# The last 128 columns of the attention tiles and of w4, computed turned

## The chip, the cores and the metric

The kernel runs on one core of a Trainium2 chip. The core has TensorE (PE) for matrix products into PSUM (8 banks of 512 float32 columns on 128 partitions), VectorE (DVE), ScalarE (ACT), GpSimd (POOL) and SyncE (SP), which here only starts transfers. The metric is the device time of one execution in microseconds (us). Three runs of the kernel before gave a median of 263.45 us (263.12 to 265.74).

## The reference

Input x has S = 2048 tokens of D = 640 features; all inputs and the output are bf16.

```
g  = sigmoid(sum(x * gate_w))                     # one number per token
q, k, v = x @ wqkv, in 32 heads of 20             # branch A
pq, pk  = phi(q), phi(k)                          # phi(t) = (t + 1 if t > 0 else exp(t)) + 1e-6
a  = (pq (pk^T v) / (pq sum(pk) + 1e-6)) @ wo
h  = gelu(layernorm(x) @ w1), shifted by 1, -1, 2, -2 tokens in four groups of features   # branch B
x1 = x + h @ w2
b  = x1 + gelu(layernorm(x1) @ w3) @ w4           # w3 is 640 x 1728, w4 is 1728 x 640
out = g * a + (1 - g) * b
```

The kernel multiplies (pk^T v) and wo into one 640 x 640 matrix M, so that branch A ends in a = pqn @ M, with pqn the scaled pq.

## The kernel before

Tokens go in 16 tiles of 128, and in 4 chunks of four tiles. The weights and x stay in SBUF. The first part makes q, k and the gate, then M; the second is w1, w2 and the two layernorms; the last part, which the change touches, is w3, the attention tiles and w4.

A matmul takes a stationary operand of up to 128 columns, loaded ahead by an instruction of its own (PEld in the profile), and streams up to 512 columns of the moving operand through it. Of a product of 640 columns that is computed with the tokens as the stationary side, 512 columns go into one PSUM bank and the last 128 into another.

- `w3_group(c, j)` makes 128 of the 1728 features of one chunk with the weights as the stationary side and 512 tokens moving; ScalarE takes the gelu into h2T (bf16, features on the partitions). 1728 is 13 x 128 + 64; the last 64 features of two chunks are made together by `w3_half` and lie in h2h, one tile on partitions 0 to 63 and the next on 64 to 127.
- `a_tile(t)` (line 1085): POOL writes (1 - g) * x1 of one tile into a slot of abx (four slots of 640 float32), TensorE makes pqn @ M for the tile with 5 matmuls of 512 columns and 5 of 128 (recorded at line 613, the helper mm_group), and one sum on VectorE (line 652) adds g times that into abx.
- `w4_half(t)` (line 1098) opens a chunk of w4: it takes three pairs of banks, one bank for the 512 columns of each of the four tiles and two banks for their last 128 columns, and writes the product of the 64 features there (lines 1115 and 1118). Two such matmuls on the lower and the upper partitions use different halves of the rows of the array.
- `w4_tile(t)` (line 1122) adds 13 matmuls of 512 and 13 of 128 columns (line 1136); two sums on VectorE (line 652) then write (1 - g) * psum + abx into x_tok, from where `out_tiles` stores groups of tiles.

The order of the program is made at build time by a planner (`_Items.run`): items stand in streams, each with things that must be placed first, a cost model says when each would be ready, and the earliest ready item goes next; among equals one that has no cost on TensorE, then the one with the longest chain of costs behind it. Each engine gets a list in that order and works through it strictly, waiting on counters of the other engines; TensorE doesn't wait for its own counter. PSUM banks are chosen at build time too, by `bank()` and `pair()`, as the ones that the cost model frees first. All transposes by DMA and nearly all stores are issued from SP's list.

In the trace the last part runs: w3 of chunks 0 and 1 with the first attention tiles in it; then for each chunk c the half block and four w4 tiles, each followed by the attention tile four ahead; between chunks stands w3 of the chunk after next. An attention tile t from 4 on is placed after w4 tile t - 4 (line 1230). The last attention tile, 15, stands between w4 tiles 14 and 15.

## Time and profile before

| | |
|---|---|
| runs of the kernel | 263.45 us median, 263.12 to 265.74 |
| the profiled execution | 262.97 us |
| its span, first to last instruction | 260.9 us |
| TensorE busy, matmuls | 257.1 us, 1651 instructions |
| VectorE, ScalarE, GpSimd busy | 149.1, 107.2, 97.3 us |
| granted TensorE clock | 1.000 |

The profile is of one execution. A row of a group names the line, the engine, the operation, output and inputs with shapes, how often it ran, busy time, mean nanoseconds of one, and the idle time before it with what ended it. A line can be that of a helper: every product made by mm_group has line 613, every sum by stt line 652. A single matmul's recorded duration (379 ns for 512 columns) includes its way through the array, which overlaps the next one; the time from one start to the next is read from the chain in order of time or from the timeline. In the chain a row is the start, the length and the work, with the number of instructions that were merged.

### The profile page before, as it was taken

The page shows a single profiled execution, that of the slowest core. Times are in us where ns is not written, and L with a number is a line of the kernel's source. Part 1 is how long each engine was busy: PE and PEld are TensorE (multiplying, and loading weights), DVE is VectorE, ACT ScalarE, POOL GpSimd, SP SyncE. Part 2 cuts the span into 40 slices and gives each one's busy share as a digit, 9 for nine tenths or more (in the row PEclk, how much of TensorE's full clock was granted, in tenths as well). Part 3 has the DMA queues.
Part 4 walks back from the last instruction along what each step waited for, and adds up shares of the span by engine and source line. Part 5 has one row for each costly group of instructions (what it writes and reads, how often), then busy time and mean ns, then how long its engine had stood idle before and what let it go on. Part 6 is the DMA issues. An engine that isn't in the chain of part 4 may idle for free.

```text
span 260.9 us, 4205 instructions
## 1 busy us (share of the span) xinstructions
PE 257.1 (99%) x1651; PEld 133.0 (51%) x1651; DVE 149.1 (57%) x267; ACT 107.2 (41%) x216; POOL 97.3 (37%) x150
## 2 busy tenths in 40 slices
PE   8999999999999999999999999999999999999996
PEld 3555555544455555555444545554455544455553
DVE  2497887899903799979993407991033410143333
ACT  1396677751365757674974240005500045100000
POOL 5013995859964017958763202320011200011000
PEclk9999999999999999999999999999999999999999
DMA  7755999652766991363585610232000020000211
GB/s 205 247 90 139 171 206 156 172 108 50 102 126 126 333 353 36 71 78 59 102 125 111 122 25 0 47 92 65 0 3 0 0 103 0 0 3 0 101 53 50
DMA packets 51283, 24.98 MB, mean 96 GB/s; under 512 B 42644, under 2 KB 49853, under 8 KB 51264
## 3 DMA queue, kind: packets, MB, share of 16 engines
q1 hardware_dynamic: 49824, 21.15, 36.8%
q0 software_dynamic: 1152, 3.28, 5.4%
q8 instruction: 13, 0.21, 0.3%
q10 hardware_dynamic: 288, 0.30, 0.3%
q14 instruction: 6, 0.05, 0.1%
HBM read 12.04 MB, written 2.62 MB: 56 GB/s over the span
## 4 chain that ended last, share of the span: by engine, by line
PE 97%; DMA 1%; DVE 1%; issue 0%
PE ps L613 61%; PE ps L1136 21%; PE ps L811 7%; PE ps L887 2%; PE ps L791 1%; DMA x_tok<-in_A_x_dram 1%; PE ps L1050 1%; PE ps L1118 1%; DVE x_tok L652 1%; PE ps L964 1%; PE ps L888 1%; PE ps L624 0%; PE ps L792 0%; DVE xT L678 0%; PE ps L1115 0%
## 5 line engine op out<-in xcount | busy, mean ns | idle before, releaser
L613 PE MATMUL ps<-xnT,w 128*128 128x512 bf16 x360 | 82.3, 379 | 0.0
L1136 PE MATMUL ps<-w,h2T 128*128 128x512 bf16 (+1 forms) x416 | 58.8, 299 | 0.0
L669 ACT ACTIVATE h2T<-ps 128x512 bf16<-128x512 f32 x52 | 30.4, 598 | 66.5 <-PE ps L613 66.5
L613 PEld LDWEIGHTS ps<-xnT,w 128*128 128x128 bf16 x360 | 34.0, 98 | 37.4 <-issue 0.4
L652 DVE SCALAR_TENSOR_TENSOR x_tok<-ps,stg,abx 128x512 bf16<-128x512 f32 (+1 forms) x32 | 17.2, 550 | 61.6 <-PE ps L1136 61.6
L635 POOL TENSOR_SCALAR abx<-x_tok,stg 128x640 f32<-128x640 bf16 x16 | 14.8, 928 | 99.6 <-DVE x_tok L652 95.1
L1136 PEld LDWEIGHTS ps<-w,h2T 128*128 128x128 bf16 x416 | 32.4, 98 | 25.6 <-issue 1.1
L635 POOL TENSOR_SCALAR xn<-x_tok,st 128x640 bf16<-128x640 bf16 x32 | 38.9, 1222 | 14.5 <-DMA xnT<-xn 14.0
L669 ACT ACTIVATE Er<-ps 128x640 bf16<-128x640 f32 x32 | 22.4, 706 | 18.1 <-PE ps L613 8.5
L668 ACT ACTIVATE junk<-x_tok 128x640 bf16<-128x640 bf16 x32 | 23.6, 738 | 3.7 <-DVE x_tok L650 3.2
L669 ACT ACTIVATE hsT<-ps 128x512 bf16<-128x512 f32 (+1 forms) x32 | 18.9, 594 | 14.7 <-PE ps L613 14.3
L613 PE MATMUL ps<-M_sb,pqnT 128*128 128x512 bf16 (+1 forms) x160 | 24.3, 299 | 0.0
L613 PE MATMUL ps<-w,hsT 128*128 128x512 bf16 (+1 forms) x160 | 23.9, 299 | 0.0
L652 DVE SCALAR_TENSOR_TENSOR abx<-ps,stg,abx 128x640 f32<-128x640 f32 x16 | 14.1, 884 | 15.8 <-PE ps L613 15.8
L613 PE MATMUL ps<-wkg,xT 128*128 128x512 bf16 (+1 forms) x150 | 22.6, 299 | 0.0
L613 PEld LDWEIGHTS ps<-w,hsT 128*128 128x128 bf16 x160 | 13.3, 98 | 12.3
L613 PEld LDWEIGHTS ps<-M_sb,pqnT 128*128 128x128 bf16 x160 | 13.1, 98 | 10.4
L613 PE MATMUL ps<-wq,xT 128*128 128x512 bf16 (+1 forms) x120 | 18.3, 299 | 0.0
L811 PE MATMUL ps<-pk_tok,x_tok 128*128 128x512 bf16 x80 | 17.8, 379 | 0.0
L650 DVE SCALAR_TENSOR_TENSOR x_tok<-ps,x_tok 128x640 bf16<-128x640 f32 x16 | 13.1, 821 | 6.9 <-PE ps L613 6.0
L635 DVE TENSOR_SCALAR Er<-Er 128x640 bf16<-128x640 bf16 x32 | 11.8, 369 | 8.6 <-ACT Er L669 8.3
L613 PEld LDWEIGHTS ps<-wkg,xT 128*128 128x128 bf16 x150 | 12.1, 97 | 9.0
(74 smaller groups left out, 236.2 us busy)
## 6 DMA issues: line engine op xcount, KB each, us to landing
w<-in_B_w_dram SPq DMA_DIRECT2D x1, 2160.0 KB, 8.2
w<-in_B_w_dram SPq DMA_DIRECT2D x1, 2080.0 KB, 14.9
x_tok<-in_A_x_dram SPq DMA_DIRECT2D x3, 640.0 KB, 5.9
out_dram<-x_tok SPq DMA_DIRECT2D x3, 640.0 KB, 3.2
w<-in_B_w_dram POOLq DMA_DIRECT2D x8, 160.0 KB, 4.8
wkg<-in_A_wqkv_dram SPq DMA_DIRECT2D x5, 160.0 KB, 4.3
wv<-in_A_wqkv_dram POOLq DMA_DIRECT2D x1, 800.0 KB, 6.4
wo_aug<-in_A_wo_dram POOLq DMA_DIRECT2D x5, 150.0 KB, 5.2
```

The lines of the kernel that those rows point to most:

```text
L613: ins = e.matmul(out_ap, l, r, start=(i == 0), stop=(i == n - 1))
L635: return engf(lambda e: e.tensor_scalar(out_ap, in_ap, s1, s2, op0, op1), rd, [out_ap], cost=cost)
L650: return dve(lambda e: e.scalar_tensor_tensor(out_ap, in0, scalar, in1, op0, op1, accum_out=accum), rd, [out_ap, accum], cost=cost + 70.0)
L652: return dve(lambda e: e.scalar_tensor_tensor(out_ap, in0, scalar, in1, op0, op1), rd, [out_ap], cost=cost)
L668: return act(lambda e: e.activation(out_ap, in_ap, func, bias=bias, scale=scale, accum_out=accum), rd, wr, cost=cost)
L669: return act(lambda e: e.activation(out_ap, in_ap, func, bias=bias, scale=scale), rd, wr, cost=cost)
L791: e.matmul(ps[:, b, :], l, x_tok[:, t, 0:512], start=(t == 0), stop=(t == NT - 1))
L811: ins = e.matmul(ps[:, b, :], l, r, start=(t0 + q_ == 0), stop=(t0 + q_ == NT - 1))
L887: e.matmul(ps[:, b, 0:512], l, w[:, k, 0:512], start=(k == 0), stop=(k == KD - 1))
L888: return e.matmul(ps[:, b + 1, 0:n2], l, w[:, k, 512:512 + n2], start=(k == 0), stop=(k == KD - 1))
L964: ins = e.matmul(o, l, r_, start=st_, stop=sp_, skip_group_check=True)
L1136: ins = e.matmul(o, l, r, start=False, stop=(i == KFF - 1), skip_group_check=(n0 > 0))
```

## The change

In all four chunks the last 128 columns of pqn @ M, and in chunks 0 to 2 the last 128 columns of w4, are made turned: the 128 columns of the weights are the stationary side and the 512 tokens of the chunk the moving one, so that the product lies in one bank with features on the partitions. ScalarE copies it to tlT as bf16 (`turn`), a DMA transpose on SP brings it to tl with tokens on the partitions, and VectorE adds the pieces: `tail_sum` for chunks 0 to 2, from tl, x_tok, g and 1 - g; `tail_add` for chunk 3, whose w4 stays as it was. `a_tile` and abx now have 512 columns and take one bank, and abx has five slots.

`w4_half` takes five single banks for a turned chunk, six single banks for the last one. For a turned chunk it issues three pieces: the 64-row product of the tail on the upper partitions (256 columns), the four of 512 columns, and the tail's on the lower partitions, which waits on TensorE's counter for the first piece, by the new argument `after`. The outputs of the two tail pieces are interleaved blocks of 128 columns in one bank. `w4_tail` then adds 13 matmuls of 512 columns ahead of the chunk's four tiles.

In the planner, the last attention tile may follow w4 tile 10 instead of 11; the turned tail of a chunk follows its last attention tile; the sums are items of a new stream.

```diff
@@ -213,10 +213,12 @@
             if any(r.lo < 0 for r in lst):
                 self.recs[space] = [r for r in lst if r.lo >= 0]
 
-    def op(self, eng, fn, reads=(), writes=(), deps=(), cost=500.0):
+    def op(self, eng, fn, reads=(), writes=(), deps=(), cost=500.0, after=None):
         d, touched, newrecs, banks = self._collect(eng, reads, writes)
         d.extend(deps)
         waits = self._waits(eng, d)
+        if after is not None:
+            waits.append((after.sem, after.val))
         self.cnt[eng] += 1
         sem = "c:" + eng
         vc = dict(self.know[eng])
@@ -515,7 +517,11 @@
     h2T = rb.alloc("h2T", [128, 2, KFF, 512], BF16)
     h2h = rb.alloc("h2h", [128, NCH, 256], BF16)
     w4 = rb.alloc("w4", [128, KFF + 1, D], BF16)
-    abx = rb.alloc("abx", [128, 4, D], F32)
+    abx = rb.alloc("abx", [128, 5, 512], F32)
+    tlT = rb.alloc("tlT", [128, 3, 512], BF16)
+    tl = rb.alloc("tl", [128, 3, 4, 128], BF16)
+    tlu = rb.alloc("tlu", [128, 4, 128], F32)
+    tlv = rb.alloc("tlv", [128, 1, 128], F32)
 
     sch.stats["sbuf"] = (pa.cur - pa.lo, pa.hi - pa.lo, ra.cur - ra.lo, rb.cur - rb.lo, ra.hi - ra.lo)
 
@@ -595,14 +601,14 @@
             cost = 150.0 + 1.2 * n
         return sch.op("pool", fn, reads, writes, cost=cost)
 
-    def pe(fn, reads, writes, cost=500.0):
+    def pe(fn, reads, writes, cost=500.0, after=None):
         for w_ in writes:
             sp_, rl = sch.rects(w_)
             if sp_ == "ps":
                 for (_p0, _p1, lo, hi) in rl:
                     for b in range(lo // PS_BANK, (hi - 1) // PS_BANK + 1):
                         bank_pend.discard(b)
-        return sch.op("pe", fn, reads, writes, cost=cost)
+        return sch.op("pe", fn, reads, writes, cost=cost, after=after)
 
     def mm_group(out_ap, pairs, reads_extra=()):
         n = len(pairs)
@@ -1081,43 +1087,105 @@
         sch.dma("sp", pqnT[:, :, 128 * t:128 * (t + 1)], pq_tok[:, t, :], "trn%d" % slot("trn", 4), transpose=True)
 
     abx_slot = {}
+    TURNED = NT - 4
 
     def a_tile(t):
-        sa = slot("abx", 4)
+        sa = slot("abx", 5)
         abx_slot[t] = sa
         tag_set("abx", sa, t)
-        ts(pool, abx[:, sa, :], x_tok[:, t, :], stg[:, 3, t:t + 1], 0.0, ALU.mult, ALU.add)
+        ts(pool, abx[:, sa, :], x_tok[:, t, 0:512], stg[:, 3, t:t + 1], 0.0, ALU.mult, ALU.add)
         tok = slice(128 * t, 128 * (t + 1))
-        b = pair()
-        mm_group(ps[:, b, 0:512], [(pqnT[:, j, tok], M_sb[:, j, 0:512]) for j in range(KD)])
-        mm_group(ps[:, b + 1, 0:128], [(pqnT[:, j, tok], M_sb[:, j, 512:D]) for j in range(KD)])
-        stt(abx[:, sa, :], psf[:, 512 * b:512 * b + D], stg[:, 2, t:t + 1], abx[:, sa, :], ALU.mult, ALU.add)
+        b = bank()
+        mm_group(ps[:, b, :], [(pqnT[:, j, tok], M_sb[:, j, 0:512]) for j in range(KD)])
+        stt(abx[:, sa, :], ps[:, b, :], stg[:, 2, t:t + 1], abx[:, sa, :], ALU.mult, ALU.add)
+
+    def turn(b, i):
+        activation(tlT[:, i, :], ps[:, b, :], ACTF.Copy)
+        sch.dma("sp", tl[:, i, :, :], tlT[:, i, :], "tl%d" % i, transpose=True)
+
+    def a_tail(c):
+        b = bank()
+        mm_group(ps[:, b, :], [(M_sb[:, j, 512:D], pqnT[:, j, 512 * c:512 * (c + 1)]) for j in range(KD)])
+        turn(b, c % 2)
+
+    def tail_add(t):
+        i = t % 4
+        ts(dve, tlu[:, i, :], x_tok[:, t, 512:D], stg[:, 3, t:t + 1], 0.0, ALU.mult, ALU.add)
+        stt(tlu[:, i, :], tl[:, t // 4 % 2, i, :], stg[:, 2, t:t + 1], tlu[:, i, :], ALU.mult, ALU.add)
+
+    def tail_sum(c):
+        xt = x_tok[:, 4 * c:4 * c + 4, 512:D]
+        tt(dve, tlu[:, :, :], tl[:, 2, :, :], xt, ALU.add)
+        for i in range(4):
+            t = 4 * c + i
+            ts(dve, tlv[:, 0, :], tl[:, c % 2, i, :], stg[:, 2, t:t + 1], 0.0, ALU.mult, ALU.add)
+            stt(x_tok[:, t, 512:D], tlu[:, i, :], stg[:, 3, t:t + 1], tlv[:, 0, :], ALU.mult, ALU.add)
 
     w4_banks = {}
 
     def w4_half(t):
         sl = (t // 4) % 2
         tag_chk("h2T", sl, t // 4)
-        b0, b2, bt = pair(), pair(), pair()
-        tiles = [((b0, b2)[i // 2] + i % 2, bt + i % 2, 128 * (i // 2)) for i in range(4)]
+        turned = t < TURNED
+        if turned:
+            bs = [bank() for _ in range(5)]
+            tiles = [(bs[i], bs[4], 128 * i) for i in range(4)]
+        else:
+            bs = [bank() for _ in range(6)]
+            tiles = [(bs[i], bs[4 + i % 2], 128 * (i // 2)) for i in range(4)]
         for i in range(4):
             w4_banks[t + i] = tiles[i]
-        bank_hold.update((b0, b0 + 1, b2, b2 + 1, bt, bt + 1))
+        bank_hold.update(bs)
+
+        def main(e, pr, par):
+            rows = slice(64 * par, 64 * par + 64)
+            bm, bs, q0 = tiles[2 * pr + par]
+            return e.matmul(ps[:, bm, :], h2h[rows, t // 4, 128 * pr:128 * (pr + 1)], w4[rows, KFF, 0:512], start=True, stop=False)
+
+        def tail(e, pr, par):
+            rows = slice(64 * par, 64 * par + 64)
+            bm, bs, q0 = tiles[2 * pr + par]
+            return e.matmul(ps[:, bs, q0:q0 + 128], h2h[rows, t // 4, 128 * pr:128 * (pr + 1)], w4[rows, KFF, 512:D],
+                            start=(pr == 0), stop=False, skip_group_check=True)
+
+        def tail_t(e, par):
+            rows = slice(64 * par, 64 * par + 64)
+            o = ps[:, bs[4], :].rearrange("p (n h q) -> p n h q", h=2, q=128)[:, :, par, :]
+            return e.matmul(o, w4[rows, KFF, 512:D], h2h[rows, t // 4, :].rearrange("p (n q) -> p n q", q=128),
+                            start=(par == 1), stop=False, skip_group_check=True)
 
         def fn(e):
             ins = None
+            if turned:
+                for i in range(4):
+                    ins = main(e, i // 2, i % 2)
+                return ins
             for pr in range(2):
-                for par, tail in ((0, False), (1, False), (0, True), (1, True)):
-                    rows = slice(64 * par, 64 * par + 64)
-                    bm, bs, q0 = tiles[2 * pr + par]
-                    l = h2h[rows, t // 4, 128 * pr:128 * (pr + 1)]
-                    if tail:
-                        ins = e.matmul(ps[:, bs, q0:q0 + 128], l, w4[rows, KFF, 512:D], start=(pr == 0), stop=False,
-                                       skip_group_check=True)
-                    else:
-                        ins = e.matmul(ps[:, bm, :], l, w4[rows, KFF, 0:512], start=True, stop=False)
+                for par, piece in ((0, main), (1, main), (0, tail), (1, tail)):
+                    ins = piece(e, pr, par)
             return ins
-        pe(fn, [h2h[:, t // 4, :], w4[:, KFF, :]], [ps[:, b, :] for b in (b0, b0 + 1, b2, b2 + 1, bt, bt + 1)], cost=760.0)
+        rd = [h2h[:, t // 4, :], w4[:, KFF, :]]
+        if not turned:
+            pe(fn, rd, [ps[:, b, :] for b in bs], cost=760.0)
+            return
+        first = pe(lambda e: tail_t(e, 1), rd, [ps[:, bs[4], :]], cost=60.0)
+        pe(fn, rd, [ps[:, b, :] for b in bs[:4]], cost=540.0)
+        pe(lambda e: tail_t(e, 0), rd, [ps[:, bs[4], :]], cost=110.0, after=first)
+
+    def w4_acc(o, prs, shared):
+        def fn(e):
+            ins = None
+            for i, (l, r) in enumerate(prs):
+                ins = e.matmul(o, l, r, start=False, stop=(i == KFF - 1), skip_group_check=shared)
+            return ins
+        pe(fn, [x_ for p_ in prs for x_ in p_], [o], cost=KFF * (nfree(o) * 0.4167 + 2.5))
+
+    def w4_tail(c):
+        tag_chk("h2T", c % 2, c)
+        b = w4_banks[4 * c][1]
+        w4_acc(ps[:, b, :], [(w4[:, k, 512:D], h2T[:, c % 2, k, :]) for k in range(KFF)], True)
+        bank_hold.discard(b)
+        turn(b, 2)
 
     def w4_tile(t):
         sa = abx_slot[t]
@@ -1126,23 +1194,16 @@
         tag_chk("h2T", sl, t // 4)
         a = t % 4
         b1, b2, q0 = w4_banks.pop(t)
-
-        def grp(o, n0, n1):
-            prs = [(h2T[:, sl, k, 128 * a:128 * (a + 1)], w4[:, k, n0:n1]) for k in range(KFF)]
-
-            def fn(e):
-                ins = None
-                for i, (l, r) in enumerate(prs):
-                    ins = e.matmul(o, l, r, start=False, stop=(i == KFF - 1), skip_group_check=(n0 > 0))
-                return ins
-            pe(fn, [x_ for p_ in prs for x_ in p_], [o], cost=KFF * ((n1 - n0) * 0.4167 + 2.5))
-        grp(ps[:, b1, 0:512], 0, 512)
-        grp(ps[:, b2, q0:q0 + 128], 512, D)
+        hs = [h2T[:, sl, k, 128 * a:128 * (a + 1)] for k in range(KFF)]
+        w4_acc(ps[:, b1, :], [(hs[k], w4[:, k, 0:512]) for k in range(KFF)], False)
         bank_hold.discard(b1)
-        if a >= 2:
-            bank_hold.discard(b2)
-        stt(x_tok[:, t, 0:512], ps[:, b1, 0:512], stg[:, 3, t:t + 1], abx[:, sa, 0:512], ALU.mult, ALU.add)
-        stt(x_tok[:, t, 512:D], ps[:, b2, q0:q0 + 128], stg[:, 3, t:t + 1], abx[:, sa, 512:D], ALU.mult, ALU.add)
+        if t >= TURNED:
+            w4_acc(ps[:, b2, q0:q0 + 128], [(hs[k], w4[:, k, 512:D]) for k in range(KFF)], True)
+            if a >= 2:
+                bank_hold.discard(b2)
+        stt(x_tok[:, t, 0:512], ps[:, b1, 0:512], stg[:, 3, t:t + 1], abx[:, sa, :], ALU.mult, ALU.add)
+        if t >= TURNED:
+            stt(x_tok[:, t, 512:D], ps[:, b2, q0:q0 + 128], stg[:, 3, t:t + 1], tlu[:, a, :], ALU.mult, ALU.add)
 
     def out_tiles(t0, t1):
         dst = out[0, 128 * t0:128 * t1, :].rearrange("(n p) d -> p n d", p=128)
@@ -1227,10 +1288,15 @@
         c = t // 4
         deps = [(("qt", t), 3.0), (("w4load",), 0.0), (("m", KD - 1), 1.0), (("mt",), 2.5)]
         if t >= 4:
-            deps.append((("w4", t - 4), 0.3))
+            deps.append((("w4", t - 5 if t == NT - 1 else t - 4), 0.3))
         else:
             deps.append((("w3", 1, t + 6), 0.0))
-        IT.add("AT", ("a", t), 1.33, lambda t=t: a_tile(t), deps)
+        IT.add("AT", ("a", t), 1.08, lambda t=t: a_tile(t), deps)
+        if t % 4 == 3:
+            IT.add("AT", ("at", c), 1.08, lambda c=c: a_tail(c), [(("qt", t), 3.0)] + ([(("ts", c - 2), 0.0)] if c >= 2 else []))
+            if t >= TURNED:
+                for u in range(t - 3, t + 1):
+                    IT.add("TS", ("ts", 100 + u), 0.0, lambda u=u: tail_add(u), deps=[(("at", c), 4.0), (("w4h", TURNED), 0.0)])
         deps4 = [(("a", t), 0.0), (("w3h", c - c % 2), GEL), (("w3", c, KFF - 1), GEL)]
         if t % 4 == 0:
             deps4.append((("w3", min(c + 1, NCH - 1), KFF - 1), 0.0))
@@ -1240,9 +1306,13 @@
             deps4.append((("a", t + 3), 0.0))
         if t % 4 == 0:
             IT.add("W4", ("w4h", t), 0.76, lambda t=t: w4_half(t), deps=deps4)
-        IT.add("W4", ("w4", t), 3.5, lambda t=t: w4_tile(t), deps=deps4)
+            if t < TURNED:
+                IT.add("W4", ("w4t", c), 2.8, lambda c=c: w4_tail(c), deps=[(("at", c), 0.0)])
+        IT.add("W4", ("w4", t), 2.8 if t < TURNED else 3.5, lambda t=t: w4_tile(t), deps=deps4 + ([(("ts", 100 + t), None)] if t >= TURNED else []))
+        if t % 4 == 2 and t < TURNED:
+            IT.add("TS", ("ts", c), 0.0, lambda c=c: tail_sum(c), deps=[(("w4", t), 0.0), (("at", c), 4.0)])
         if t in OUT_AT:
-            IT.add("OUT", ("out", t), 0.0, lambda t=t: out_tiles(OUT_AT[t], t + 1), deps=[(("w4", t), 0.0)])
+            IT.add("OUT", ("out", t), 0.0, lambda t=t: out_tiles(OUT_AT[t], t + 1), deps=[(("w4", t), 0.0)] + ([(("ts", c), 0.0)] if t < TURNED else []))
 
     hook = None
     if stop == "A":

```

## The prediction

> **What bounds the kernel now.** First the page's head, its table of busy shares and its chain of work.
>
> ```profile
> span 260.9 us, 4205 instructions
> PE 257.1 (99%) x1651; PEld 133.0 (51%) x1651; DVE 149.1 (57%) x267; ACT 107.2 (41%) x216; POOL 97.3 (37%) x150
> PE 97%; DMA 1%; DVE 1%; issue 0%
> ```
>
> TensorE is busy all the time and the chain runs through it, so only what shortens or delays the row of matmuls counts. A busy PE need not be a fast one, so I read the same chain in order of time, where one step is the time from start to start. Here is chunk 1 of the last stage, with one row of wide matmuls alone and the last row.
>
> ```profile
> 56.83 13.81 PE ps L811 x64
> ...
> 173.24 15.39 PE ps L613 x75
> 188.62 0.32 PE ps L1118 x2
> 188.95 0.06 PE ps L1115 x2
> 189.00 0.22 PE ps L1118 x2
> 189.22 0.06 PE ps L1115 x2
> 189.27 3.64 PE ps L1136 x26
> 192.91 1.36 PE ps L613 x10
> 194.27 3.53 PE ps L1136 x26
> ...
> 257.67 1.08 DVE x_tok L652 x2
> ```
>
> A 512-column matmul costs 13.81 / 64 = 0.2158 us. A tile of the last product has 13 wide and 13 narrow ones: 3.53 / 13 - 0.2158 = 0.0557 for a narrow one. An attention tile (L613 x10) gives 1.36 / 5 - 0.2158 = 0.056. So four narrow matmuls take 0.223 and one wide one 0.2158: the columns are what is paid for, and 128 of them are nearly as cheap as a quarter of 512. Does a narrow matmul wait for its weights? The groups by shape:
>
> ```profile
> L1136 PE MATMUL ps<-w,h2T 128*128 128x512 bf16 x208 | 47.5, 379 | 0.0
> L1136 PEld LDWEIGHTS ps<-w,h2T 128*128 128x128 bf16 x416 | 32.4, 98 | 25.6 <-issue 1.1
> L1136 PE MATMUL ps<-w,h2T 128*128 128x128 bf16 x208 | 14.2, 219 | 0.0
> L613 PE MATMUL ps<-M_sb,pqnT 128*128 128x128 bf16 x80 | 7.1, 219 | 0.0
> ```
>
> A load is recorded at 98 ns, more than 0.0557; but the pair of a wide and a narrow matmul keeps the pace of its columns, so two loads (0.196) lie beside one pair (0.2715). There is no load time to win.
>
> **The change, part by part.** *Turned tails.* In all four chunks the 4 x 5 narrow attention matmuls become 5 wide ones: 20 fours. In three chunks the 4 x 13 narrow ones of w4 become 13 wide: 39 fours. That is 59 x (4 x 0.0557 - 0.2158) = 59 x 0.007 = 0.41 us saved. With 0.056 for a narrow one it is 0.49, with a rounding error of 0.005 in the 3.53 it is 0.32. I take 0.41.
>
> The Trainium skill, in "TensorE: Matmul & The Clock Gate", section Back-to-back issue gap, says otherwise: in a stream of load and matmul pairs it gives about 81 ns at 128 columns and 131 ns at 512. By it a four would save 4 x 81 - 131 = 193 ns and the sum would be 11.4 us; the trace has 0.056 and 0.216 in their place and disagrees with both figures.
>
> *The half block (64 rows).* Before, two matmuls on different row halves run side by side: 0.22 + 0.06 + 0.22 + 0.06 (with 0.10 of entry in the first figure). After, a tail of 256 columns on the upper rows goes first, then four wide ones alternating lower and upper, then a tail on the lower rows. A 256-column matmul isn't in the trace; between 0.056 and 0.216 I take half the wide one, 0.108. Each row half then has 0.216 + 0.216 + 0.108 = 0.54 against 0.544 before. If row halves overlap when they are started one by one, this is nothing; if nothing overlaps, it is 4 x 0.216 + 2 x 0.108 = 1.08, or 0.54 more, 1.6 for three chunks. I take nothing: the weight loads below run in pairs ahead for both halves, so the halves are already served separately.
>
> ```profile
> 173.07 1.52 PE L613 MATMUL ps<-M_sb,pqnT 128*128 128x512 bf16 x10
> ...
> 188.55 0.10 PEld L1118 LDWEIGHTS ps<-w,h2h 64*128 64x128 bf16 x2 [0.42 <-ACT h2T L669]
> 188.56 0.39 PE L1118 MATMUL ps<-w,h2h 64*128 64x512 bf16 x2
> 188.57 0.10 PEld L1115 LDWEIGHTS ps<-w,h2h 64*128 64x128 bf16 x2
> ...
> 238.23 3.69 PE L1136 MATMUL ps<-w,h2T 128*128 128x512 bf16 x26
> 242.04 0.10 PEld L1118 LDWEIGHTS ps<-w,h2h 64*128 64x128 bf16 x2 [0.29 <-DVE x_tok L652]
> ...
> 254.66 3.69 PE L1136 MATMUL ps<-w,h2T 128*128 128x512 bf16 x26
> 257.67 1.08 DVE L652 SCALAR_TENSOR_TENSOR x_tok<-ps,stg,abx 128x512 bf16<-128x512 f32 x2 [1.92 <-PE ps L1136]
> ```
>
> The tail's output is in two runs of 128 columns with a step between them. The Trainium skill, "PSUM — Partial Sum Buffer", section Specifications, says that any non-contiguous output slows matmuls significantly; no run here shows a stepped output, and at double time the six tails would cost 0.65 us.
>
> *The added wait.* The second tail waits on TensorE's own counter for the first. Behind it on PE stand its weight load, its matmul and the 13 wide matmuls of the turned w4 tail; ScalarE's copy waits for those. From the rows at 254.66 and 257.67: 13 wide matmuls have streamed at 254.66 + 13 x 0.2158 = 257.46, and VectorE, which waits for them, starts 0.21 later. So the wait opens 0.108 + 0.21 = 0.32 after the block starts, the load (0.095, the 0.10 of the row) is done at 0.41, and the matmul is due when its row half is free, at 0.43. Covered with 0.02 to spare; without cover it costs up to the 0.21 each time, 0.6 in all. I take nothing, and keep 0.6 for the range.
>
> *Entry into the half block of chunk 3.* In chunk 1 the wide run ends at 173.07 + 15.39 = 188.46 and the block starts at 188.56, a gap of 0.10. ScalarE isn't it, whatever the row names: the matmuls before the block use all 128 rows and these use 64, and the way back has 0.10 too (189.05 + 0.056 to 189.21). That stays, as many changes of form remain. In chunk 3 the row ends at 238.23 + 3.53 = 241.76 and the block starts at 242.04: 0.28, and there VectorE really ends last, since three even pairs of banks were asked for and one held the tile just finished. After, six single banks are taken, those free first, so the youngest can be left out, and the tail that went with it is long copied: 0.18 saved.
>
> *Moved step.* The last attention tile goes from before w4 tile 15 to before w4 tile 11, and the turned tail of chunk 3 with it. They pass one w4 tile, the half block and three tiles on PE; on POOL one scaling, on VectorE one sum, on SP one transpose. The work on PE is the same wherever it stands. The fifth slot of sums carries the earlier start. The end keeps its form: w4 tile 15 stays with wide and then narrow matmuls, then two sums (the 1.08 above), then the store: nothing.
>
> *Added work off the path.* Seven copies on ScalarE, seven transposes on SP, and on VectorE a sum of 4 x 128 columns and eight small operations for each turned chunk, eight for the last.
>
> ```profile
> L669 ACT ACTIVATE hsT<-ps 128x512 bf16<-128x512 f32 x16 | 9.5, 598 | 10.5 <-PE ps L613 10.4
> L652 DVE SCALAR_TENSOR_TENSOR abx<-ps,stg,abx 128x640 f32<-128x640 f32 x16 | 14.1, 884 | 15.8 <-PE ps L613 15.8
> L643 DVE TENSOR_TENSOR qprod<-pq_tok,zb 128x640 f32<-128x640 bf16 x16 | 13.1, 816 | 0.0
> L652 DVE SCALAR_TENSOR_TENSOR x_tok<-ps,stg,abx 128x512 bf16<-128x512 f32 x16 | 12.0, 750 | 61.6 <-PE ps L1136 61.6
> L652 DVE SCALAR_TENSOR_TENSOR x_tok<-ps,stg,abx 128x128 bf16<-128x128 f32 x16 | 5.6, 350 | 0.0
> L635 DVE TENSOR_SCALAR dnr<-dnr 128x32 f32<-128x32 f32 x16 | 3.3, 203 | 0.1
> ...
> pqnT<-pq_tok SPq DMA_TRANSPOSE x16, 2.6
> ...
> SPq L286 <- DVE x_tok L652: 78.4, 5, 34.0
> ...
> 163.50:168.40 4.90, 4.90 (x38) 2.77 (x36) 4.78 (x11) 0.00 (x0) 1.31 (x1) 1.00 0.18 33
> ...
> 173.20:188.60 15.40, 15.40 (x78) 6.95 (x77) 4.11 (x9) 7.17 (x12) 1.30 (x1) 1.00 0.24 64
> 188.60:207.60 19.00, 19.00 (x144) 10.64 (x144) 6.58 (x10) 0.60 (x1) 2.41 (x3) 1.00 0.00 1
> ```
>
> (The last three rows: stretch, then busy time of PE, weight loads, VectorE, ScalarE and POOL.) A copy is 0.6 on a ScalarE that is idle in the w4 stretches. A transpose lands after 2.6, and its sums are read some 10 us later; SP stands waiting 78 us for finished tiles there, so the store behind a transpose is not delayed by what it can feel. VectorE: the sum is 0.65 (512 / 640 of 0.816), a small operation between 0.2 and 0.35, say 0.3: 0.65 + 8 x 0.3 = 3.05, against 4 x 0.35 + 4 x (0.884 - 0.750) = 1.94 taken away. In chunks 1 to 3 that lies in over 12 free us. Chunk 0 is the tight place, see below. Cost: nothing, so long as TensorE finds banks.
>
> **Sum:** -0.41 - 0.18 = -0.59. The profiled execution has 262.97 (260.9 and 2.07 around it): 262.4. The median of the runs shown is 0.48 higher, at 263.45, with the lowest at 263.12; from the median it would be 262.9. I forecast the middle, **262.6**, with 262.0 to 263.3 as its own range.
>
> **Rivals.**
> (a) *The half blocks lose their side-by-side run.* For it: no matmuls of unequal length alternate between row halves in this trace, the stepped output is new, and the wait has 0.02 to spare. Against: the paired loads. Place: the starts of w4 in chunks 0, 1, 2. Price up to 0.54 each, 1.6 together: 262.6 + 1.6 = 264.2, slower than before. From 0.2 lost in each block (0.59 / 3) the change loses. Chance 0.14.
> (b) *VectorE becomes the bound in chunk 0.* A w4 tile with its attention tile shrinks from 4.90 to 13 x 0.2158 + 1.08 = 3.89 on PE, while VectorE's 4.78 only falls by 0.33 + 0.13 to 4.3; three tiles leave it 1.3 behind, and the sum of chunk 0 adds 3.05: 4.4 late when w3 of chunk 2 begins. Then up to four of eight banks (two attention tiles, two w4 tiles) still wait for it, and w3 needs two at a time (1.08 each, evacuated in 0.6): enough, and VectorE catches up in a stretch where it has 4.11 of 15.40. It decides only if over six banks wait; then TensorE pays about three of the 4.4: 265.6. Chance 0.05.
> (c) *The order comes out otherwise* (the planner keeps the last attention tile late, or the six banks include the youngest): the 0.18 is not won, 262.8. Chance 0.09.
> (d) *Weight loads bind narrow matmuls after all.* If a narrow matmul cost its load, 0.098, the fours would give 59 x (0.392 - 0.216) = 10.4: 252.2. The 3.53 row would then be 4.08. Chance 0.02; this is what the skill's pair figures amount to.
>
> **How the numbers follow.** Forecast 0.70, (a) 0.14, (b) 0.05, (c) 0.09, (d) 0.02. The range goes down to 261.9 (0.49 and 0.18 from the profiled execution, with 0.4 for the scatter of runs) and up to 264.2, which takes in (a) whole and (c). Over 1% is 2.6 us, about what a measurement of this kernel can tell from no change; faster by that takes (d): 0.02. Slower by that takes (b) at more than its price, or (a) and (b) together: 0.05. The rest, 0.93, is within it.
>
> **What would show it.** Wide w4 groups of 13 at 2.80 and narrow rows at L613 only before the last stage; the half block 0.54 to 0.66 from its first start to the next 128-row matmul (a: over 0.85); a start gap of 0.10 at chunk 3; no wait of PE on VectorE; the end row still 1.08. The forecast is wrong if PE shows waits behind the second tail, or if w3 of chunk 2 takes over 15.4 with its attention tile.

## The result, and the profile after

The changed kernel takes 262.39 us (median, 262.05 to 264.02) and the kernel before, measured with it, 263.37 (262.86 to 265.74). The medians differ by 0.98 us. The ratio is 0.9964, with a 95% interval from 0.9952 to 0.9977: 0.95 us faster, between 0.6 and 1.3. The profiled execution of the changed kernel took 262.39 us, with a span of 260.7. First the head of its page, the busy shares and the chain by engine.

```profile
span 260.7 us, 3891 instructions
PE 257.0 (99%) x1468; PEld 126.2 (48%) x1468; DVE 155.5 (60%) x290; ACT 111.3 (43%) x223; POOL 95.4 (37%) x150
PE 97%; DMA 1%; DVE 1%; issue 0%
```

TensorE is still the bound, with 183 matmuls fewer and nearly the same busy time: 0.1 us less. The spans differ by 0.2 only, because this execution lost 0.4 at the start: the first tile of x landed 0.07 later (2.91 for 2.84 in the two chains), and the first products, behind it, took longer (five transposes 0.55 for 0.29). So one needs a mark behind the start. I take the first of the twenty matmuls that make pk^T v's product with the weights (lines 964 and 970), which both kernels have at the same place. The chain in order of time, start and length, for the kernel before:

```profile
77.12 1.05 PE ps L964 x20
...
154.28 0.32 PE ps L1118 x2
...
222.97 0.32 PE ps L1118 x2
```

and for the changed kernel:

```profile
77.56 1.05 PE ps L970 x20
...
154.68 0.21 PE ps L1154
...
155.33 5.72 PE ps L1179 x26
161.05 1.08 PE ps L619 x5
162.13 2.81 PE ps L1179 x13
...
172.70 16.19 PE ps L619 x75
188.89 0.21 PE ps L1154
...
223.10 0.21 PE ps L1154
...
237.23 3.24 PE ps L619 x15
...
257.47 1.08 DVE x_tok L658 x2
```

From the mark to the last sums it was 257.67 - 77.12 = 180.55, and it is 257.47 - 77.56 = 179.91: **0.64 less**. By stretches: up to the first half block 77.16 and 77.12 (0.04), chunk 0 34.34 and 34.21 (0.13), chunk 1 34.35 and 34.21 (0.14), the rest 34.70 and 34.37 (0.33). A w4 tile is one row of 2.81 where it was 3.53, an attention tile 1.08 where it was 1.36, and the turned w4 tail with the first tile is the 5.72. The row of 16.19 is w3 of a chunk with its attention tile and the turned tail of the next one: 75 wide matmuls at 0.2158, where the 15.39 had 70 wide and 5 narrow.

Most of the rest of the 0.98 lies outside the span. Over all runs the median span went from 261.3 to 260.7, and the time around the span from 2.07 to 1.74, in each kernel the same to about 0.1. That 0.33 has experiments of its own below.

The half block of chunk 0 in the timeline of the changed kernel:

```profile
154.61 0.09 PEld L1154 LDWEIGHTS ps<-h2h,w 64*128 64x128 bf16 x1 [0.42 <-ACT h2T L675]
154.61 0.22 PEld L1143 LDWEIGHTS ps<-w,h2h 64*128 64x128 bf16 x4
154.61 0.28 PE L1154 MATMUL ps<-h2h,w 64*128 64x256 bf16 x1
154.62 0.71 PE L1143 MATMUL ps<-w,h2h 64*128 64x512 bf16 x4
...
154.95 0.09 PEld L1154 LDWEIGHTS ps<-h2h,w 64*128 64x128 bf16 x1
155.06 0.27 PE L1154 MATMUL ps<-h2h,w 64*128 64x256 bf16 x1
155.26 0.55 PEld L1179 LDWEIGHTS ps<-h2T,w 128*128 128x128 bf16 x4 [0.21 <-issue]
```

The first wide matmul starts 0.01 after the first tail, on the other row half; the four and the second tail fit into 0.65 until the next 128-row work (154.61 to 155.26), as before in chunk 1, where the block starts at 188.56 and the next row is

```profile
189.21 2.98 PE L1136 MATMUL ps<-w,h2T 128*128 128x512 bf16 x13
```

Work of unequal length on the two row halves does run side by side.

### The profile page after: what moved, and what is told of

The parts are those of the page before. It is cut to its first block, busy times and chain, and to the rows that moved or that the text cites. A ratio compares the mean times of both kernels' runs of the same rounds, so it can differ in the third digit from the quotient of the medians.

```text
span 260.7 us, 3891 instructions
## 1 busy us (share of the span) xinstructions
PE 257.0 (99%) x1468; PEld 126.2 (48%) x1468; DVE 155.5 (60%) x290; ACT 111.3 (43%) x223; POOL 95.4 (37%) x150
## 4 chain that ended last, share of the span: by engine, by line
PE 97%; DMA 1%; DVE 1%; issue 0%
PE ps L619 61%; PE ps L1179 21%; PE ps L817 7%; PE ps L893 2%; PE ps L797 1%; DMA x_tok<-in_A_x_dram 1%; PE ps L1056 1%; PE ps L1143 1%; PE ps L630 1%; PE ps L894 1%; PE ps L970 1%; DVE x_tok L658 0%; PE ps L798 0%; PE ps L1154 0%; DVE xT L684 0%
## 5 line engine op out<-in xcount | busy, mean ns | idle before, releaser
L1179 PE MATMUL ps<-w,h2T 128*128 128x512 bf16 (+1 forms) x260 | 49.9, 347 | 0.0
L658 DVE SCALAR_TENSOR_TENSOR x_tok<-ps,stg,abx 128x512 bf16<-128x512 f32 x16 | 12.0, 749 | 59.2 <-PE ps L1179 59.2
L641 POOL TENSOR_SCALAR xn<-x_tok,st 128x640 bf16<-128x640 bf16 x32 | 39.8, 1251 | 13.9 <-DMA xnT<-xn 13.5
L641 POOL TENSOR_SCALAR abx<-x_tok,stg 128x512 f32<-128x512 bf16 x16 | 12.8, 800 | 86.0 <-DVE x_tok L658 69.0
L1179 PEld LDWEIGHTS ps<-w,h2T 128*128 128x128 bf16 x260 | 23.3, 98 | 24.8 <-issue 0.3
L675 ACT ACTIVATE tlT<-ps 128x512 bf16<-128x512 f32 x7 | 4.2, 597 | 55.7 <-PE ps L619 46.8
L619 PE MATMUL ps<-M_sb,pqnT 128*128 128x512 bf16 x80 | 19.7, 379 | 0.0
L658 DVE SCALAR_TENSOR_TENSOR abx<-ps,stg,abx 128x512 f32<-128x512 f32 x16 | 11.9, 747 | 10.2 <-PE ps L619 7.5
```

The source lines that it names most:

```text
L619: ins = e.matmul(out_ap, l, r, start=(i == 0), stop=(i == n - 1))
L641: return engf(lambda e: e.tensor_scalar(out_ap, in_ap, s1, s2, op0, op1), rd, [out_ap], cost=cost)
L658: return dve(lambda e: e.scalar_tensor_tensor(out_ap, in0, scalar, in1, op0, op1), rd, [out_ap], cost=cost)
L675: return act(lambda e: e.activation(out_ap, in_ap, func, bias=bias, scale=scale), rd, wr, cost=cost)
L1179: ins = e.matmul(o, l, r, start=False, stop=(i == KFF - 1), skip_group_check=shared)
```

## The experiments

All times below are medians, unless a run is said to have been timed once. "From the mark" is the time from the twenty matmuls at lines 964 to 971 to the start of the last sums in the profiled execution; it was 180.55 before and is 179.91 in the changed kernel. It repeats far better than the whole time: two later runs of the kernel before, with nothing but waits added to lists other than TensorE's, have 180.55 and 180.54, and four later runs that lose nothing on TensorE have 179.91 each.

**Attention turned alone.**

```diff
-    TURNED = NT - 4
+    TURNED = 0
```

(with the items of the tails' sums made to follow each chunk's own half block)

> Only the attention tails are turned, in all four chunks; w4 stays narrow in all 16 tiles, its last columns added from the transposed attention tail by the sums that chunk 3 has in the changed kernel. Theory (fewer columns' worth of matmul starts, 0.007 us per four): against the changed kernel 39 fours of w4 go back, 39 x 0.007 = +0.27 us, so 0.67 below the kernel before where the changed one is 0.94 below; in the trace the w4 rows are 3.53 again and an attention tile 1.08. Rival (narrow matmuls bound by their weight loads, 98 ns): 39 x (0.392 - 0.216) = +6.9. Rival (the gain is in launch or code size, not in the matmuls): time outside the span goes back towards the 2.07 of the kernel before, from 1.69, while the span hardly moves.

Measured: 262.73 us, ratio 0.9973 (0.9957 to 0.9989), 0.34 above the changed kernel; time around the span 1.72. The chain in order of time:

```profile
78.45 1.05 PE ps L970 x20
...
233.08 1.08 PE ps L619 x5
234.16 3.53 PE ps L1179 x26
...
258.66 1.08 DVE x_tok L658 x2
```

From the mark 180.21: 0.30 of the 0.64 is given back, for 0.27 expected, and a w4 tile has its 3.53 again, an attention tile the 1.08. The rival by weight loads (6.9 us) is out, and so is a gain that comes with the number of matmuls launched: with 1640 instructions in TensorE's list the time around the span is the changed kernel's.

**The tails of the half block side by side in time.** In `w4_half` the second tail is issued right behind the first:

```diff
         first = pe(lambda e: tail_t(e, 1), ...)
-        pe(fn, rd, [ps[:, b, :] for b in bs[:4]], cost=540.0)
         pe(lambda e: tail_t(e, 0), ..., after=first)
+        pe(fn, rd, [ps[:, b, :] for b in bs[:4]], cost=540.0)
```

> In the half block of the turned chunks both tail matmuls come first, with the wait of the second on the first right between them, then the four wide ones. Theory (the wait opens 0.32 after the block's start and a load of 0.095 follows; in the changed kernel it is covered by the four wide ones): the second tail starts at about 0.41, the wide ones at 0.52, the next 128-row matmul at 1.05 from the block's start against 0.65, +0.4 for each of three blocks, +1.2 us against the changed kernel, so about 0.3 above the kernel before. Rival (TensorE's wait for its own counter is free): the block stays 0.65 and the time that of the changed kernel.

Measured: 263.40 us, ratio 0.9997 (0.9986 to 1.0009), 1.01 above the changed kernel. The timeline of the block in chunk 0:

```profile
154.43 0.62 PE L1154 MATMUL ps<-h2h,w 64*128 64x256 bf16 x2
154.76 0.09 PEld L1154 LDWEIGHTS ps<-h2h,w 64*128 64x128 bf16 x1 [0.25 <-PE ps L1154]
154.77 0.70 PE L1143 MATMUL ps<-w,h2h 64*128 64x512 bf16 x4
...
155.41 0.11 PEld L1179 LDWEIGHTS ps<-h2T,w 128*128 128x128 bf16 x2 [0.42 <-issue]
```

The wait opens 0.33 after the first start (0.32 expected), and the whole block takes 0.98 in place of 0.65: 0.33 each, three times. The 0.33 is a little less than the 0.40 expected, since the matmul starts 0.01 behind the start of its weight load, not behind its 0.095. So the added wait costs 0.33 where nothing covers it, and in the changed kernel, with the four wide matmuls ahead, nothing that can be seen.

**The half block of chunk 3 with pairs of banks.**

```diff
-            bs = [bank() for _ in range(6)]
+            bs = [q + i for q in (pair(), pair(), pair()) for i in range(2)]
```

> The half block of chunk 3 takes three even pairs of banks as in the kernel before, all else as changed. Theory (a pair held the bank of the tile just finished, and single banks leave it out): the gap ahead of that block is 0.28 again instead of 0.10 and the time +0.18 us against the changed kernel. Rival (the gap went because the last attention tile and the turned tail moved ahead of it): the gap stays 0.10 and the time too.

Measured: 262.39 us, ratio 0.9966 (0.9951 to 0.9982): the changed kernel's time, and from the mark 257.37 - 77.46 = 179.91. Its timeline has the block's start at 243.11, behind a wide row that started at 240.21 and so ended at 243.01:

```profile
240.21 2.97 PE L1179 MATMUL ps<-w,h2T 128*128 128x512 bf16 x13
...
243.11 0.39 PE L1143 MATMUL ps<-w,h2h 64*128 64x512 bf16 x2
```

The gap is 0.10, so the expectation was wrong: pairs as such don't bring the 0.28 back. In the kernel before, w4 tile 11 was on two pairs, one for its wide columns and one for its narrow ones, and three of four pairs could not leave both out. Here its last columns are long copied and only one pair is young. With attention alone turned, single banks and narrow tails in chunk 2 gave 0.10 as well (its block starts at 244.39, behind a w4 tile that started at 240.76 and ended at 240.76 + 3.53 = 244.29). So single banks do it with narrow tails, and turned tails do it with pairs. In both of these runs the last attention tile stood ahead of the block, so neither shows that it can do without that. The move alone should not be enough: with pairs and narrow tails w4 tile 11 lies in two of the four pairs, and the block takes three. No run tests that.

**The last attention tile late.**

```diff
-            deps.append((("w4", t - 5 if t == NT - 1 else t - 4), 0.3))
+            deps.append((("w4", t - 4), 0.3))
```

> The last attention tile may again only follow w4 tile 11, all else as changed. Theory (work on TensorE costs the same wherever it stands, banks set the gap): within 0.1 us of the changed kernel, gap ahead of the half block of chunk 3 0.10, with the attention tile and the turned tail of chunk 3 behind it. Rival (the moved step is what won the 0.18, or its late transpose holds up the first sums of chunk 3): +0.2 us or more, with a wait of TensorE or a later end row.

Measured: 263.08 us, ratio 0.9983 (0.9968 to 0.9998), 0.69 above the changed kernel, so the expectation was wrong. Time around the span: 1.96, 0.22 more. From the mark 257.86 - 77.53 = 180.33: 0.42 more. The chain in order of time leaves TensorE here:

```profile
234.39 2.82 PE ps L1179 x13
237.24 0.75 DVE x_tok L658
237.99 0.60 DVE tlu L649
...
240.62 0.30 DVE tlv L641
240.97 0.23 issue
241.21 0.75 DVE abx L658
241.96 0.14 issue
242.10 0.81 PE ps L619 x3
```

and the list of waits has TensorE on VectorE, which the changed kernel's has not:

```profile
PE ps L619 <- DVE abx L658: 0.4, 1, 0.4
```

VectorE takes the tails' sums of chunk 2 (238 to 241.2) ahead of the sum of attention tile 14 at 241.21, whose product was done at 238.11. Until then that bank is held; the half block of chunk 3 holds six; and the last attention tile, now behind that block, stands until 242.10 for a bank: the only other one has w4 tile 11, whose sum comes after that of attention tile 14. The gap ahead of the block itself is 0.10 here too (the row from 238.11 has streamed at 240.92, the block starts at 241.01), with single banks and turned tails together. The wait list of the kernel before doesn't show its gap of 0.28 either, so an empty list speaks only of longer waits.

**The same, with those sums later in VectorE's list.** On top of the last edit:

```diff
-            IT.add("TS", ("ts", c), ..., deps=[(("w4", t), 0.0), (("at", c), 4.0)])
+            IT.add("TS", ("ts", c), ..., deps=[(("w4", t), 0.0), (("at", c), 4.0)]
+                   + ([(("w4h", TURNED), 0.0), (("a", NT - 1), 0.0)] if c == 2 else []))
```

> The last attention tile late as in the run with the late attention tile (263.08, of which 0.22 lies around the span, at 187 instructions of GpSimd), but the sums of chunk 2's tails stand in VectorE's list behind the last attention tile's sum, not ahead of the sum of attention tile 14; TensorE's order is the same. Theory (TensorE waited 0.46 us there for the bank of attention tile 14, held by VectorE, which was at those sums): no wait of TensorE on VectorE and 0.46 us less span, 262.6. Rival (the late transpose or the order on TensorE costs it): 263.1 again.

Measured: 262.82 us, ratio 0.9982 (0.9958 to 1.0005), time around the span 1.92. From the mark 257.75 - 77.84 = 179.91, the changed kernel's to the last digit; its list of waits has none of TensorE on VectorE for a bank of the last part. So what the moved step is worth is that bank, 0.42 us, by keeping the attention tile ahead of the block that takes six; with the sums behind it, the late tile costs nothing. The ratio's interval alone can't tell these two late kernels apart; the traces do.

**VectorE loaded in chunk 0.** Sums that repeat the first one of `tail_sum`, 9 or 24 of them, for c = 0:

```diff
         xt = x_tok[:, 4 * c:4 * c + 4, 512:D]
+        for _ in range(9 if c == 0 else 0):
+            tt(dve, tlu[:, :, :], tl[:, 2, :, :], xt, ALU.add)
```

> Nine more sums of 4 x 128 columns on VectorE (0.68 us each, 6.1 in all) ahead of the sums of chunk 0, all else as changed. In the changed kernel VectorE is 5.0 us late at the last w4 tile of chunk 0 (sum at 177.69, product done at 172.7). Theory (TensorE pays only when a bank is asked for that VectorE still holds): the sum of attention tile 7 moves from 179.93 to about 186, before the half block of chunk 1 at 188.9 asks for five banks, so TensorE loses nothing: span as changed, 0 to 0.1. Rival (a late VectorE costs at once): several us.

> The same with 24 more sums, 16.3 us. Theory: the sums of attention tile 6, w4 tile 3 and attention tile 7 move to about 192, 194 and 196, behind the half block of chunk 1 at 188.9; three of eight banks are then held by VectorE and two by ScalarE's last copies until about 190.3, the block needs five, so it starts about 1.4 us later, with a wait of TensorE there, and the span is 1.4 us longer. Rival (banks are never short): nothing. Rival (a late VectorE is paid in full): over 10 us.

Measured, one time each: 264.07 us with 9, but from the mark 259.13 - 79.22 = 179.91, nothing lost; this execution began 1.7 later than the changed kernel's. With 24: 262.72 us, from the mark 257.78 - 77.12 = 180.66, 0.75 lost. The timeline of the second at chunk 1:

```profile
188.49 0.60 ACT L675 ACTIVATE h2T<-ps 128x512 bf16<-128x512 f32 x1 [0.48 <-PE ps L619]
...
189.14 0.28 PE L1156 MATMUL ps<-h2h,w 64*128 64x256 bf16 x1 [0.69 <-ACT h2T L675]
...
192.62 0.74 DVE L658 SCALAR_TENSOR_TENSOR abx<-ps,stg,abx 128x512 f32<-128x512 f32 x1
...
194.81 0.74 DVE L658 SCALAR_TENSOR_TENSOR x_tok<-ps,stg,abx 128x512 bf16<-128x512 f32 x1
...
197.06 0.74 DVE L658 SCALAR_TENSOR_TENSOR abx<-ps,stg,abx 128x512 f32<-128x512 f32 x1
```

Three banks wait for VectorE until 192.6 and later, the block needs five, and it waits for one that ScalarE has just copied, 0.69. I had counted one bank more as taken (1.4 expected). The mechanism held, and the size was half of what I expected: a late VectorE costs nothing until a bank is missing, nothing with 6 us of extra load and 0.75 with 16.

**All four chunks turned.**

```diff
-    TURNED = NT - 4
+    TURNED = NT
```

> The last chunk of w4 is turned as well. Theory: 13 fours fewer, 0.09 us less on TensorE; but now the last wide group ends the row of matmuls, and what follows it is 0.21 until VectorE starts and a sum of 0.75, 0.96 in all, where before the narrow group (0.72) ran beside that sum and only 0.59 followed the last matmul: 0.37 more. Together +0.28 against the changed kernel, about 262.7. Rival (the end is not set by VectorE): -0.1.

Measured: 266.15 us, ratio 1.0093 (1.0064 to 1.0122), 3.8 above the changed kernel. The timeline's end:

```profile
258.35 0.75 DVE L658 SCALAR_TENSOR_TENSOR x_tok<-ps,stg,abx 128x512 bf16<-128x512 f32 x1 [2.05 <-PE ps L1179]
259.02 0.68 DVE L649 TENSOR_TENSOR tlu<-tl,x_tok 128x512 f32<-128x512 bf16 x1
...
262.06 0.35 DVE L658 SCALAR_TENSOR_TENSOR x_tok<-tlu,stg,tlv 128x128 bf16<-128x128 f32 x1
```

The planner placed the tails' sums of chunk 3 behind the last tile's own sum, and all nine stand behind the last matmul. I had not seen that they would. The start of the last tile's own sum, 258.35 - 77.82 = 180.53 from the mark, is that of the next run (180.54), so what is lost lies behind it. With those sums behind w4 tile 12:

> All four chunks of w4 turned, with the sums of the last chunk's tails placed behind w4 tile 12 instead of behind the last tile. In the run with all chunks turned these sums (2.96 us on VectorE) stood behind the last tile's own sum and made it 3.8 longer. Theory: that is gone, 0.09 less on TensorE by 13 fours, 0.37 more at the end (0.21 and a sum of 0.75 behind the last matmul, in place of 0.59): +0.28 against the changed kernel, from the first wide row of matmuls to the last sum's start +2.6 (the narrow group of 0.72 no longer follows). Rival (VectorE's sums still end last): +1 or more.

Measured: 262.90 us, ratio 0.9981 (0.9958 to 1.0003); 0.51 above the changed kernel. From the mark to the end of the last sum 259.08 + 0.75 - 78.54 = 181.29, against 179.91 + 1.08 = 180.99 in the changed kernel: 0.30, for 0.28 expected. Leaving the last chunk as it was is worth that; the rest of the 0.51 isn't in the work from the mark on.

**The time around the span.** Waits for counters that have long reached their value were added to the engines' lists: one at the end of GpSimd's list in the changed kernel; in the kernel before as many on GpSimd's as to make its length the changed kernel's; and then the same on SyncE's, ScalarE's and VectorE's too, two thirds down the lists. Where several stand together, two entries of the code make one instruction.

```diff
+            self.prog["pool"].append(([("d:tl0", 16)], None, None))
```

> One more wait, long fulfilled, at the end of GpSimd's list, all else as changed. Over all runs the time around the span is 2.07 us for the kernel before and 1.74 for the changed one, each within 0.1; that is 0.33 of the 0.98 by which the medians differ. The late attention tile's run had 1.96, with one more instruction on GpSimd. Theory A (it depends on how many instructions stand in GpSimd's list, 183 before, 186 after, 187 there): 1.96 here. Theory B (it depends on another list, or on the kernel's end): 1.74 here. The span stays as changed either way.

```diff
+            for i_ in range(6):
+                self.prog["pool"].append(([("d:x%d" % (i_ % 3), 16)], None, None))
```

> The kernel before, with three more instructions in GpSimd's list (waits that are long fulfilled, at its end), so that it has the 186 of the changed kernel in place of 183. Theory A (the 0.33 around the span hangs on where GpSimd's list ends): time around the span 1.74 in place of 2.07, span as before, time 0.33 below the kernel before, 0.9987. Theory B (another list, or the work at the kernel's end): 2.07 and no difference.

```diff
+            for e_, n_ in (('sp', 16), ('act', 22), ('dve', 48)):
+                at_ = len(self.prog[e_]) * 2 // 3
+                self.prog[e_][at_:at_] = [([("d:x%d" % (i_ % 3), 16)], None, None) for i_ in range(n_)]
```

> The kernel before with long fulfilled waits added to four lists, so that GpSimd, SyncE, ScalarE and VectorE have as many instructions as in the changed kernel (186, 128, 225, 322 in place of 183, 120, 214, 298); TensorE's list stays at 1698 against 1521. With GpSimd's alone the time around the span stayed at 2.10. Theory A (the 0.33 around the span hangs on the length of one of the lists of SyncE, ScalarE or VectorE, not on what the kernel does): 1.74 around the span, span as before or a little longer by the waits, time 0.3 below the kernel before. Theory B (TensorE's list, or the kernel's own end): 2.07 to 2.10, time as before.

Measured (instructions in the lists, and the time less the span; the changed kernel with one wait more was timed once, at 262.94 us, with 257.79 - 77.88 = 179.91 from the mark):

| kernel | GpSimd | SyncE | ScalarE | VectorE | TensorE | around the span, us |
|---|---|---|---|---|---|---|
| before | 183 | 120 | 214 | 298 | 1698 | 2.07 |
| before, GpSimd's list longer | 186 | 120 | 214 | 298 | 1698 | 2.10 |
| before, four lists longer | 186 | 128 | 225 | 322 | 1698 | 1.70 |
| changed | 186 | 128 | 225 | 322 | 1521 | 1.74 |
| changed, one wait more | 187 | 128 | 225 | 322 | 1521 | 1.94 |
| last attention tile late | 187 | 127 | 224 | 324 | 1521 | 1.96 |
| late, with later sums | 187 | 127 | 225 | 324 | 1521 | 1.92 |
| all chunks turned | 186 | 129 | 227 | 318 | 1479 | 1.76 |
| attention alone turned | 185 | 124 | 219 | 337 | 1640 | 1.72 |

The kernel before with four longer lists took 262.89 us, 0.9967 (0.9948 to 0.9986) of the kernel before, and from the mark it has 258.47 - 77.93 = 180.54, as before. Its median is 0.6 below that of the kernel before, of which 0.41 (2.11 to 1.70, beside the same runs) lies around the span and the rest in the scatter of the spans' starts. So empty waits alone win 0.3 to 0.4 us, a third or more of what the change wins. GpSimd's length alone doesn't bring 2.07 down (263.36 us, 0.9997), but it can bring 1.74 up to 1.94. So more than one list counts. Which of SyncE's, ScalarE's and VectorE's holds the kernel before at 2.07, and whether it goes by their lengths or by what stands where in them, stays open.

## Why the prediction was right, point by point

*The bound.* TensorE's row of matmuls was read as the only thing that counts. From the mark the change is -0.64, for -0.59 forecast, and in the medians of the spans -0.6. One of the prediction's signs of being wrong was set wrong: w3 of chunk 2 takes 16.19, over its 15.4, since the turned tail's five wide matmuls (1.08) now stand in that row; without them it is 15.11.

*Turned tails:* 0.41 forecast, about 0.44 measured. With attention alone turned, the w4 share is 0.30 (0.27 forecast); what stands before the first half block and in chunks 0 and 1 (0.04, 0.13, 0.14) is what 5 and 18 fours of 0.007 give (0.035, 0.13, 0.13). The pair figures of the Trainium skill ("TensorE: Matmul & The Clock Gate", section Back-to-back issue gap) don't hold in this kernel: rows of 13 wide matmuls with their loads take 2.81, or 0.216 each, not 131 ns, rows of 13 narrow ones 0.72, or 0.056 each, not 81 ns, and a four turned is worth 0.007, not the 0.193 that an estimate from those figures gives.

One reading behind this term was wrong, though its conclusion holds: the narrow matmuls of w4 don't lie in pairs with wide ones, where two loads share 0.2715. The kernel issues 13 wide ones and then 13 narrow ones, and the loads of such a narrow row in the kernel before are

```profile
157.68 0.71 PEld L1136 LDWEIGHTS ps<-w,h2T 128*128 128x128 bf16 x12
```

Twelve loads recorded at 98 ns each, 1.18 in all, lie within 0.71: they overlap one another, and so don't hold a narrow row back even where no wide matmul covers them. So the trace of the kernel before already spoke against rival (d).

*The half block:* nothing forecast, nothing measured (0.65 and 0.65). Rival (a) falls: unequal matmuls on the two row halves overlap. The slowing by a non-contiguous output (the Trainium skill, "PSUM — Partial Sum Buffer", section Specifications) doesn't show in this trace: the last tail starts 0.45 after the block, and at the double time that the prediction priced, 0.216, with the 0.10 of the way back, the next row would come at about 0.76; it comes at 0.65.

*The added wait:* forecast to open at 0.32 and to be covered. It opens at 0.33, and uncovered it costs 0.33 a block; the prediction's bound of 0.21 was too small. In the changed kernel the second tail's load starts at 154.95, 0.34 behind the block's start, and its matmul at 155.06, when its row half is free; since a matmul can start 0.01 behind its load, there was 0.1 to spare, not the 0.02 of the prediction.

*Entry into the half block of chunk 3:* 0.18 forecast. The last stretch lost 0.33, of which the turned tails of chunk 2 and of the last attention tiles explain 18 x 0.007 = 0.13; 0.20 is left, and the gap is 0.10 for 0.28. In the changed kernel w4 tile 11 starts at 240.30 and has streamed at 240.30 + 2.81 = 243.11:

```profile
240.30 1.03 PE L1179 MATMUL ps<-w,h2T 128*128 128x512 bf16 x4
...
243.21 0.39 PE L1143 MATMUL ps<-w,h2h 64*128 64x512 bf16 x2
```

The size was right. The reason was more than was needed: the prediction asked for single banks and the early copied tail, and either does it without the other, with the attention tile moved ahead.

*Moved step:* here the prediction was wrong without harm. "The work on PE is the same wherever it stands" leaves out banks. With the tails' sums on VectorE, a late last attention tile costs 0.42; moved ahead it doesn't come to that. Rival (c) priced the late tile at the 0.18 of the block's gap; it costs more, and at another place, since that gap stays 0.10.

*Added work off the path:* forecast free, and free. The sizes, in the groups of the changed kernel:

```profile
L658 DVE SCALAR_TENSOR_TENSOR x_tok<-tlu,stg,tlv 128x128 bf16<-128x128 f32 x12 | 4.4, 370 | 0.4
L641 DVE TENSOR_SCALAR tlv<-tl,stg 128x128 f32<-128x128 bf16 x12 | 4.3, 359 | 0.3
L675 ACT ACTIVATE tlT<-ps 128x512 bf16<-128x512 f32 x7 | 4.2, 597 | 55.7 <-PE ps L619 46.8 <-PE ps L1179 8.9
L649 DVE TENSOR_TENSOR tlu<-tl,x_tok 128x512 f32<-128x512 bf16 x3 | 2.0, 682 | 0.0
```

A turned chunk's sums are 0.68 + 4 x (0.36 + 0.37) = 3.6 by these durations, which overlap at their ends (170.37 to 173.99, 3.6, in chunk 0), for 3.05 forecast. VectorE was 5.0 late at the end of chunk 0 (in its timeline the sum of w4 tile 3 starts at 177.69, the product was done at 172.7), for 4.4 forecast. Rival (b) named the right mechanism and the wrong place: in chunk 0 it takes more than 6 us of extra work, and no more than 16, to cost anything, and at the end of chunk 2, three microseconds are enough once the last attention tile is late.

*From the sum to the time.* The sum gave 262.4 from the profiled execution, and that is the result, but the agreement is luck. The profiled execution of before was a quick one to start: 262.97, 0.40 below the median of 263.37. And the sum kept the 2.07 around the span as it was, without a word on why, and there 0.33 went. From the median the same sum gives 262.8. So the 0.85 between 263.45 and the forecast of 262.6 comes near the 0.95 measured by luck too: the reasons given carry 0.6.

## What to carry to other kernels

Where TensorE runs without gaps, price a reshaped product by its columns from start to start; turning narrow matmuls into wide ones saved some 7 ns per four here, 0.44 us in all. Its side effects were not small beside that: 0.2 for a bank that comes free earlier, and 0.42 that a late attention tile would cost for where the sums stand in VectorE's list. When work goes to an engine off the path, look not at its busy share but at which banks wait in its list, and at the next place that asks for many banks at once. And before a third of a microsecond is put down to the work, compare the spans: here a third of the gain lay around the span, and empty waits in the kernel before won as much.

## What the runs showed of the hardware that was not expected

The time around the span depends on the engines' instruction lists, also where the work on TensorE stays the same: it came out at 1.70 to 1.76, at 1.92 to 1.96 or at 2.07 to 2.11 us in these runs; waits added to four lists took it from 2.11 to 1.70, and in the one execution with one wait more on GpSimd it was 1.94 for 1.74. TensorE's wait for its own counter opens 0.33 us after the start of a 256-column matmul, and its next matmul starts 0.01 behind the start of its weight load. A change between work on 128 rows and on 64 costs 0.10 us each way (188.46 to 188.56 and 189.11 to 189.21 in the kernel before). Weight loads recorded at 98 ns overlap one another in a row of narrow matmuls (twelve in 0.71 us). The start of an execution scatters: the mark lay between 77.12 and 79.22 in these profiles, with the same work ahead of it in each, while the time from the mark on repeats to 0.01 where TensorE loses nothing.
